# Reordering the softmax's VectorE work and the weight conversion in a fused attention and expert kernel

## The chip, the cores and the metric

One core of one Trainium2 chip runs the whole kernel in one launch. The metric is the device time of an execution in microseconds (us); the kernel before took 818.86 us, the median of three runs (818.68 to 821.95).

## The reference

Three parts, in fp32: a windowed attention, a mixture of experts with one expert per token, and a dense layer pair with g = h - tanh(h). Shapes: q, k, v are (4, 8, 576, 64); 2304 tokens of width 512; 8 experts of inner width 1024; the last pair has an inner width of 2048.

```python
# attention: each row sees itself and the 63 rows before it
scores = scale * np.matmul(q, k.transpose(0, 1, 3, 2))
scores = np.where(mask, scores, -1000000000.0)
scores = scores - np.max(scores, axis=-1, keepdims=True)
attn = np.exp(scores)
attn = attn / (np.sum(attn, axis=-1, keepdims=True) + 1e-09)
x = np.matmul(attn, v)                      # then (B*S, H*D)
# experts
logits = x @ w_gate + modality_bias[modality_id]
e_idx = np.argmax(logits, axis=1)           # gate_w = softmax(logits)[e_idx]
out[mask] = gate_w[mask, None] * (np.maximum(x[mask] @ w1[e], 0.0) @ w2[e])
# last pair; its weights come as float64
h = x @ w_in
return (h - np.tanh(h)) @ w_out
```

## The kernel before

The instructions are issued in the order in which the Python code runs (a manual schedule); each engine works through its own queue in that order and waits at the head for what it needs. SP issues the direct DMAs, one queue in order.

**Attention.** `attention` (L370) runs an iteration for each of 36 groups g of four 128x128 score blocks, nine per batch, as a software pipeline: in iteration g TensorE gets the transposes of q and k for a later group (`prep`, every second group), the scores of group g+2 (`stS`), the transposes of the probabilities of group g (`stT`) and the product with v of group g-1 (`stV`). In `stS` VectorE takes the row maxima nm of a group from PSUM (L314) and ScalarE computes four exponentials into P with the row sums as an accumulator output (L316; the trace shows each as an ACTIVATE and an ACTIVATION_READ_ACCUMULATOR). In `stN` VectorE adds 1e-9 to the sums (smm, L323) and takes the reciprocal rc (L324), and GpSimd multiplies P by it (L325). In `stT` four transposes go into ps_t, a PSUM pool with one buffer, and PT is copied out by ScalarE for odd g (L335) and by VectorE for even g (L337). The score pool has two buffers, P three. The routing of a finished batch (`route_task`) and the rows for the experts (`xrow_task`) are generators; `Sched.pump` moves every waiting one a step, once per iteration.

**Conversion.** `conv_task` (L698) is one more generator, driven by `conv_step`: it turns the float64 weights of the last pair into two fp32r parts, in 32 tiles. Of each tile ScalarE converts the low words (`conv_low`, L767), VectorE does four operations on the high words (`conv_top`, L757 to L760), GpSimd adds the two (`conv_sum`, L773), and the sum is split by ScalarE (L778) and a VectorE subtraction (L782). Ten tiles (NWA) are converted in attention, the split of each in the steps of the next tile; the others in the expert loop, when ScalarE does the first of the four operations (L755).

**Routing table.** After the last batch `unit_table` (L605) computes on VectorE where each expert's tokens lie. It ends with a flag okB, a 1x1 value that TensorE multiplies by ones (L691) to bring it to 128 partitions; VectorE reads the product (L692 to L695: okc, no, slot). The product uses `xps`, the ring of PSUM buffers that the transposes of gathered tokens (`xsplit`, L838) use too, two buffers in this stage. okc and slot are read only by `out_ids` (L940).

**Expert loop.** `moe` (L957) runs 40 steps p, eight inner slices f for each of five units of tokens. A step loads and splits weights (`wload`, `wsplit`), runs the first layer for slice f (`l1`) and the second for f-1 (`l2`), pumps the generators twice and steps the conversion up to twice, for p from CONV0 = 3 and f from 1 to 6. `xsplit` for the next unit stands in the step with f = 7. At p = N - 7 the conversion's buffers are closed and those for the first chunk of the last stage are opened; `ychunk` then loads it through the ring r, which the weights use too. `second` is the last stage.

Of the kernel before, what the change touches and what calls it, by code (L numbers as in the profile page):

```python
# [8 lines left out]
F32 = mybir.dt.float32  # L9
F32R = mybir.dt.float32r  # L10
BF16 = mybir.dt.bfloat16
I32 = mybir.dt.int32
ALU = mybir.AluOpType
AF = mybir.ActivationFunctionType
AX = mybir.AxisListType
# [26 lines left out]
NWA = 10  # L42
NWB = 7
CONV0 = 3
CONVF = (1, 2, 3, 4, 5, 6)
GATHER0 = 2
XACT = 11
# [28 lines left out]
class Kernel:  # L76
# [218 lines left out]
    def stS(self, g):  # L295
        nc = self.nc
        b, hp, half = self.gl(g)
        ps = self.psS.tile([128, 4, 128], F32, name="ps_s")
        mask = self.mF if half == 0 else self.mG
        nc.tensor.matmul(  # L300
            ps.rearrange("p a b -> p (a b)"), self.idB, mask.rearrange("p a b -> p (a b)"), start=True, stop=True
        )
        for j in range(4):
            if hp is None:
                lhs, rhs = self.qbt[:, j, :], self.kTt[b % 2][:, j, :]
            else:
                i = 4 * half + j
                w = 64 * max(i - 1, 0)
                lhs, rhs = self.qbd[(b * 4 + hp) % 2][:, i, :], self.kT[(b * 4 + hp) % 2][:, w : w + 128]
            nc.tensor.matmul(ps[:, j, :], lhs, rhs, start=False, stop=True, skip_group_check=True)  # L310
        nm = self.at.tile([128, 4], F32, name="nm", bufs=3)
        sm = self.at.tile([128, 4], F32, name="smm", bufs=3)
        P = self.at.tile([128, 4, 128], F32, name="P", bufs=3)
        nc.vector.tensor_reduce(nm, ps, op=ALU.max, axis=AX.X, negate=True)  # L314
        for j in range(4):
            nc.scalar.activation(P[:, j, :], ps[:, j, :], AF.Exp, bias=nm[:, j : j + 1], accum_out=sm[:, j : j + 1])  # L316
        self.grp[g] = [P, sm, None]

    def stN(self, g):
        nc = self.nc  # L320
        P, sm, _ = self.grp[g]
        rc = self.at.tile([128, 4], F32, name="rc", bufs=3)
        nc.vector.tensor_scalar(sm, sm, 1e-9, None, op0=ALU.add)  # L323
        nc.vector.reciprocal(rc, sm)  # L324
        nc.gpsimd.tensor_tensor(P, P, rc[:, :, None].to_broadcast([128, 4, 128]), op=ALU.mult)  # L325

    def stT(self, g):
        nc = self.nc
        P = self.grp[g][0]
        pt = self.psT.tile([128, 4, 128], F32, name="ps_t")  # L330
        for j in range(4):
            nc.tensor.transpose(pt[:, j, :], P[:, j, :], self.idF)  # L332
        PT = self.at.tile([128, 4, 128], F32, name="PT", bufs=2)
        if g % 2:
            nc.scalar.activation(PT, pt, AF.Copy)  # L335
        else:
            nc.vector.tensor_copy(PT, pt)  # L337
        self.grp[g][2] = PT

    def stV(self, g):  # L340
# [29 lines left out]
    def attention(self):  # L370
        NG = 9 * B
        self.load_qk(0)
        self.consts()
        for t in self.qbd + [self.qbt]:
            self.nc.vector.memset(t, 0.0)
        self.consts_route()
        self.load_v(0)
        self.load_qk(1)
        self.prep(0)
        for g in range(-2, NG + 2):  # L380
            n = g + 3
            self.useZ = g < NG
            if 0 < n < NG:
                b, i = divmod(n, 9)
                if i < 8 and i % 2 == 0:
                    pi = 4 * b + i // 2
                    self.prep(pi)
                if i == 5:
                    self.prep_tail(b)
                if n == 1:  # L390
                    self.sched.add(self.consts_gate())
                if n == 4:
                    self.conv = self.conv_task()
                if i < 8 and i % 2 == 1:
                    pi = 4 * b + i // 2
                    self.shift_v(pi)
                    if pi + 2 < 4 * B:
                        self.load_qk(pi + 2)
                    if pi + 1 < 4 * B:
                        self.load_v(pi + 1)  # L400
            if 0 <= g + 1 < NG:
                self.stN(g + 1)
            if 0 <= g + 2 < NG:
                self.stS(g + 2)
            if 0 <= g < NG:
                self.stT(g)
            if 0 <= g - 1 < NG:
                self.stO(g - 1, self.stV(g - 1))
                if (g - 1) % 9 == 8:
                    self.sched.add(self.route_task((g - 1) // 9))  # L410
            if g >= NG - 2:
                u, f = self.units["E", 0], g - NG + 2
                if f < 3:
                    self.wload(u, f, 1)
                if f >= 2:
                    self.wload(u, f - 2, 2)
                if f == 2:
                    self.wsplit(u, 0, 1)
            self.sched.pump()
            if g % 3 != 2 or g < 6:  # L420
                self.conv_step()


# [181 lines left out]
    def unit_table(self):  # L605
        nc, rt = self.nc, self.rt
        v = nc.vector
# [3 lines left out]
        n = self.counts("nB")  # L611
# [14 lines left out]
        g = rt.tile([1, NLIST, E], F32, name="le")[:, :E]  # L626
# [59 lines left out]
        self.fin = fin  # L686
        okB = rt.tile([1, 1], BF16, name="okB")
        v.tensor_scalar(okB, over, float(NSTAT), None, op0=ALU.is_le)
        yield 2
        ps = self.xps([128, 1])  # L690
        nc.tensor.matmul(ps, self.ones[0:1, :], okB, start=True, stop=True)  # L691
        v.tensor_copy(self.okc, ps)  # L692
# [5 lines left out]
    def conv_task(self):  # L698
        tiles = [(0, f) for f in range(NF2)] + [(1, f) for f in range(NF2)]
        ready = lambda w, f: (f < NWA or self.conv_on) if w == 0 else f < len(self.woutH) or self.woutW  # L700
        raws, late = [self.conv_load(*t) for t in tiles[:2]], None
        for _ in range(5):
            yield
        for i, (w, f) in enumerate(tiles):
            while not ready(w, f):
                yield
            cur = raws.pop(0)
            r = self.conv_low(cur)
            if i < NWA:
                if late:  # L710
                    hl = self.split_hi(*late)
                yield
                if late:
                    self.split_lo(hl, late[2])
                a = self.conv_top(cur, False)
            else:
                a = self.conv_top(cur, True)
                if late:
                    self.split(*late)
                yield  # L720
            late = self.conv_sum(w, f, a, r)
            if i + 2 < len(tiles):
                raws.append(self.conv_load(*tiles[i + 2]))
            yield
        if late:
            self.split(*late)
        self.conv_done = True
# [17 lines left out]
            nc.sync.dma_start(raw, ap["wout"].bitcast(I32)[f * 128 : f * 128 + 128, :])  # L745
        return raw

    def conv_top(self, raw, act):

        hi = raw.rearrange("p (n two) -> p n two", two=2)[:, :, 1]  # L750
        a = self.cv.tile([128, 512], I32, name="cva")
        v, x = self.nc.vector, a.bitcast(F32)
        hf = raw.bitcast(F32).rearrange("p (n two) -> p n two", two=2)[:, :, 1]
        if act:
            self.nc.scalar.activation(x, hf, AF.Abs)  # L755
        else:
            v.tensor_scalar(a, hi, 0x7FFFFFFF, None, op0=ALU.bitwise_and)  # L757
        v.tensor_scalar(x, x, bits(0x38000000), bits(0x47EFFFFF), op0=ALU.max, op1=ALU.min)
        v.tensor_scalar(a, a, 0x07FFFFFF, 3, op0=ALU.bitwise_and, op1=ALU.logical_shift_left)
        v.scalar_tensor_tensor(a, hi, -0x40000000, a, op0=ALU.bitwise_and, op1=ALU.bitwise_or)  # L760
        return a

    def conv_low(self, raw):
# [193 lines left out]
    def moe(self):  # L957
        order = [("E", j) for j in range(NEARLY)] + list(range(NSTAT))
        seq = [(u, f) for u in order for f in range(NF1)]
        N = len(seq)  # L960
# [5 lines left out]
        for p in range(N):  # L966
            self.conv_on = True
            i, f = p // NF1, p % NF1
# [5 lines left out]
            u, g = at(p + 3)  # L974
# [4 lines left out]
            u, g = at(p + 2)  # L979
            if u is not None:  # L980
                self.wload(u, g, 2)
            u, g = at(p + 1)
            if u is not None:
                self.wsplit(u, g, 1)
            u, f = at(p)
# [6 lines left out]
            elif p == N - 4:  # L992
                self.sched.add(self.out_ids())
            self.sched.pump()
            if f in CONVF and p >= CONV0:
                self.conv_step()
            if f:
                if f == NF1 - 1 and p + 1 < N:
                    self.xsplit(U[seq[p + 1][0]], 2)
                self.l2(u, f - 1)  # L1000
            self.sched.pump()
            if f in CONVF and p >= CONV0:
                self.conv_step()
            if f == NF1 - 1:
                if p + 1 < N:
# [3 lines left out]
            if 1 <= f <= 4 and i > 0 or p == N - 1:  # L1009
                j = i - (p < N - 1)  # L1010
# [3 lines left out]
            if p == NF1 + 1:  # L1014
# [4 lines left out]
                self.woutH += [wc.tile([128, DM], F32R, name=f"woutH{f}") for f in range(NWB, half)]  # L1019
                self.woutL += [wc.tile([128, DM], F32R, name=f"woutL{f}") for f in range(NWB, half)]  # L1020
                self.woutW = [wc.tile([128, DM], I32, name=f"woutW{f}") for f in range(half)]
            if p == N - 7:
                assert not self.conv
                self.es_cv.close()
                y0, self.es_y0 = self.pool("y0", 1)
                self.ybuf = [self.ytiles(y0, 0)]
                self.yc = {}
                self.sched.add(self.ychunk(0, self.mo, "r"))
# [277 lines left out]
def bits(x):  # L1306
    return struct.unpack("<f", struct.pack("<I", x))[0]
# [35 lines left out]
```

## Time and profile before

| | before |
|---|---|
| median of three runs | 818.86 us |
| the profiled execution | 820.09 us, its span 818.3 us |
| TensorE (PE) busy | 763.6 us, 93% of the span |
| VectorE (DVE) busy | 638.6 us, 78% |
| ScalarE (ACT) busy | 527.6 us, 64% |
| GpSimd (POOL) busy | 262.4 us, 32% |

The profile is one execution. Busy time is the union of an engine's instructions; PEld, the weight loads, overlaps PE. A line L314 is line 314 of the kernel. An idle time in brackets is that of the engine just before the instruction, with the instruction that ended it. A row of the windows view gives a stretch, its length, then the busy time of PE, PEld, VectorE, ScalarE and GpSimd in this order. The granted clock is a mean over a stretch, 1.00 being 2.4 GHz. Attention lasts until about 160 us, the expert loop from about 171 to 402 us, and the last stage to the end.

### The profile page before, as it was taken

The page shows a single profiled execution, that of the slowest core. Times are in us where ns is not written, and L with a number is a line of the kernel's source. Part 1 is how long each engine was busy: PE and PEld are TensorE (multiplying, and loading weights), DVE is VectorE, ACT ScalarE, POOL GpSimd, SP SyncE. Part 2 cuts the span into 40 slices and gives each one's busy share as a digit, 9 for nine tenths or more (in the row PEclk, how much of TensorE's full clock was granted, in tenths as well). Part 3 has the DMA queues.
Part 4 walks back from the last instruction along what each step waited for, and adds up shares of the span by engine and source line. Part 5 has one row for each costly group of instructions (what it writes and reads, how often), then busy time and mean ns, then how long its engine had stood idle before and what let it go on. Part 6 is the DMA issues. An engine that isn't in the chain of part 4 may idle for free.

```text
span 818.3 us, 13365 instructions
## 1 busy us (share of the span) xinstructions
PE 763.6 (93%) x4462; PEld 658.5 (80%) x4478; DVE 638.6 (78%) x1137; ACT 527.6 (64%) x1250; POOL 262.4 (32%) x271
## 2 busy tenths in 40 slices
PE   7798889789789999999899999999999999999995
PEld 5677676657578888889889999999999999999993
DVE  4658687756968788775499888888888888888883
ACT  4867676735445565545588777777777767777772
POOL 4333333520105142331024343323424423334223
PEclk9999999899989999999999999999999999999998
DMA  6867867455338586664400010100101101000001
GB/s 137 200 164 179 208 157 200 147 171 174 111 104 262 179 240 203 196 192 144 134 1 29 10 40 10 30 14 26 40 1 40 33 7 39 21 2 26 14 1 42
DMA packets 114543, 80.38 MB, mean 98 GB/s; under 512 B 66141, under 2 KB 102511, under 8 KB 114465
## 3 DMA queue, kind: packets, MB, share of 16 engines
q1 hardware_dynamic: 111201, 69.81, 30.1%
q0 software_dynamic: 3264, 9.63, 3.8%
q8 instruction: 37, 0.61, 0.3%
q14 instruction: 41, 0.34, 0.1%
HBM read 62.10 MB, written 14.16 MB: 93 GB/s over the span
## 4 chain that ended last, share of the span: by engine, by line
PE 79%; DVE 8%; ACT 5%; DMA 3%; issue 2%; POOL 1%; SPq 0%; POOLq 0%; ACTq 0%; DVEq 0%
PE ps_g L1155 24%; PE ps_q L1198 23%; PE ps_h L880 10%; PE ps_y L897 10%; ACT P L316 2%; PE ps_s L310 2%; DMA qr<-in_q 2%; PE ps_o L354 1%; PE ps_t L332 1%; PE x L838 1%; PE x L453 1%; DVE nm L314 1%; PE z L453 1%; DMA r<-yd 1%; PE x L430 1%
## 5 line engine op out<-in xcount | busy, mean ns | idle before, releaser
L1186 POOL TENSOR_TENSOR gl<-gv,gh 128x384 fp32r<-128x384 f32 x96 | 99.8, 1039 | 214.6 <-ACT gh L1185 214.2
L1155 PE MATMUL ps_g<-yh,winH 128*128 128x384 f32 x384 | 129.6, 338 | 2.0 <-DVE gt L1176 2.0
L1155 PE MATMUL ps_g<-yl,winH 128*128 128x384 f32 x384 | 129.6, 337 | 0.0
L1155 PE MATMUL ps_g<-yh,winL 128*128 128x384 f32 x384 | 129.3, 337 | 0.0
L1177 DVE COPY_PREDICATED gv<-gm,gt 128x384 f32<-128x384 int32 x96 | 109.4, 1139 | 10.2 <-ACT gu L1167 0.5
L1198 PE MATMUL ps_q<-woutH,gl 128*128 128x512 f32 x288 | 113.5, 394 | 1.0 <-POOL gl L1186 1.0
L1198 PE MATMUL ps_q<-woutL,gh 128*128 128x512 f32 x288 | 113.5, 394 | 0.0
L1198 PE MATMUL ps_q<-woutH,gh 128*128 128x512 f32 x288 | 113.0, 392 | 0.1
L1185 ACT ACTIVATE gh<-gv 128x384 fp32r<-128x384 f32 x96 | 50.3, 524 | 96.8 <-issue 81.9
L1173 DVE SCALAR_TENSOR_TENSOR gv<-gu,ps_g 128x384 f32<-128x384 f32 x96 | 53.1, 553 | 36.7 <-ACT gt L1170 36.2
L1155 PEld LDWEIGHTS ps_g<-yh,winH 128*128 128x128 f32 x384 | 72.1, 188 | 6.6 <-DVE gt L1176 2.6
L1155 PEld LDWEIGHTS ps_g<-yl,winH 128*128 128x128 f32 x384 | 72.1, 188 | 3.8
L1175 DVE SCALAR_TENSOR_TENSOR gv<-gs,gv 128x384 f32<-128x384 f32 x96 | 72.4, 755 | 3.3
L773 POOL TENSOR_TENSOR cvw<-cva,cvr 128x512 int32<-128x512 int32 x24 | 36.0, 1498 | 114.8 <-DVE winL L782 50.8
L316 ACT ACTIVATE P<-ps_s,nm 128x128 f32<-128x128 f32 x144 | 51.0, 371 | 33.3 <-DVE nm L314 30.9
L1155 PEld LDWEIGHTS ps_g<-yh,winL 128*128 128x128 f32 x384 | 72.1, 188 | 0.0
L1198 PEld LDWEIGHTS ps_q<-woutL,gh 128*128 128x128 f32 x288 | 54.0, 188 | 12.2
L1198 PEld LDWEIGHTS ps_q<-woutH,gl 128*128 128x128 f32 x288 | 54.1, 188 | 10.5 <-POOL gl L1186 1.7
L1168 ACT ACTIVATE gs<-gu,pa 128x384 f32<-128x384 f32 x96 | 59.3, 618 | 4.4 <-DVE gv L1174 1.2
L1174 DVE SCALAR_TENSOR_TENSOR gv<-gs,gv 128x384 f32<-128x384 f32 x96 | 58.8, 612 | 3.3
L1198 PEld LDWEIGHTS ps_q<-woutH,gh 128*128 128x128 f32 x288 | 54.0, 188 | 9.1 <-ACT gh L1185 0.5
L1169 ACT ACTIVATE gs<-gu,pa 128x384 f32<-128x384 f32 x96 | 57.9, 604 | 3.5 <-DVE gv L1175 3.5
(263 smaller groups left out, 1653.9 us busy)
## 6 DMA issues: line engine op xcount, KB each, us to landing
r<-in_w SPq DMA_DIRECT2D x80, 256.0 KB
raw<-in_win SPq DMA_DIRECT2D x16, 512.0 KB
raw<-in_wout SPq DMA_DIRECT2D x16, 512.0 KB
xs<-r SPq DMA_DIRECT2D x18, 256.0 KB
kr<-in_k SPq DMA_DIRECT2D x32, 128.0 KB
qr<-in_q SPq DMA_DIRECT2D x32, 128.0 KB
va<-in_v SPq DMA_DIRECT2D x32, 128.0 KB
yd<-ys SPq DMA_DIRECT2D x16, 252.0 KB
```

The lines of the kernel that those rows point to most:

```text
L316: nc.scalar.activation(P[:, j, :], ps[:, j, :], AF.Exp, bias=nm[:, j : j + 1], accum_out=sm[:, j : j + 1])
L880: nc.tensor.matmul(ps, w[:, c, :], x[:, c, :n], start=(c == 0 and i == 0), stop=(c == 3 and i == 2))
L897: nc.tensor.matmul(u.y[d], w[:, d * 128 : d * 128 + 128], x, start=(f == 0 and i == 0), stop=(f == NF1 - 1 and i == 2),)
L1155: nc.tensor.matmul(ps, w[:, c, :], x[:, c, :], start=(c == 0 and i == 0), stop=(c == 3 and i == 2))
L1168: nc.scalar.activation(s1, u, AF.Square, bias=self.pa1)
L1169: nc.scalar.activation(s2, u, AF.Square, bias=self.pa2)
L1173: nc.vector.scalar_tensor_tensor(v, u, cA, ps, op0=ALU.mult, op1=ALU.mult)
L1174: nc.vector.scalar_tensor_tensor(v, s1, b1, v, op0=ALU.add, op1=ALU.mult)
L1175: nc.vector.scalar_tensor_tensor(v, s2, b2, v, op0=ALU.add, op1=ALU.mult)
L1177: nc.vector.copy_predicated(v, m.bitcast(I32), t)
L1186: nc.gpsimd.tensor_tensor(gl, v, gh.bitcast(F32), op=ALU.subtract)
L1198: nc.tensor.matmul(self.po[t], g[:, sl], w, start=(f == 0 and i == 0), stop=(f == NF2 - 1 and i == 2))
```

## The change

In `attention` the scores of group g+2, with their maxima and exponentials, are issued ahead of the sums of group g+1; the conversion is stepped once between `stN` and `stT` of every iteration, and at the end of an iteration when g is not a multiple of 4 (before: at the end of two in three). For the first ten tiles `conv_top` is issued in two parts in two steps, and the split in two steps of the same tile. The exponentials have no accumulator output; `stN` sums P with one VectorE reduction. PT is always copied by ScalarE. `unit_table` waits 14 pumps instead of 2 before it multiplies the flag. In the expert loop the conversion is not stepped at p = 9 and 10, and also at f = 0 from the third unit on; its buffers are closed one step later.

```diff
@@ stS, stN, stT
-            nc.scalar.activation(P[:, j, :], ps[:, j, :], AF.Exp, bias=nm[:, j : j + 1], accum_out=sm[:, j : j + 1])
+            nc.scalar.activation(P[:, j, :], ps[:, j, :], AF.Exp, bias=nm[:, j : j + 1])
...
+        nc.vector.tensor_reduce(sm, P, op=ALU.add, axis=AX.X)
         nc.vector.tensor_scalar(sm, sm, 1e-9, None, op0=ALU.add)
...
-        if g % 2:
-            nc.scalar.activation(PT, pt, AF.Copy)
-        else:
-            nc.vector.tensor_copy(PT, pt)
+        nc.scalar.activation(PT, pt, AF.Copy)
@@ attention
+            if 0 <= g + 2 < NG:
+                self.stS(g + 2)
             if 0 <= g + 1 < NG:
                 self.stN(g + 1)
-            if 0 <= g + 2 < NG:
-                self.stS(g + 2)
+            self.conv_step()
             if 0 <= g < NG:
                 self.stT(g)
...
-            if g % 3 != 2 or g < 6:
+            if g % 4:
                 self.conv_step()
@@ unit_table
-        yield 2
+        yield 14
         ps = self.xps([128, 1])
@@ conv_task
             if i < NWA:
-                if late:
-                    hl = self.split_hi(*late)
+                a = self.conv_top(cur, False, 1)
                 yield
-                if late:
-                    self.split_lo(hl, late[2])
-                a = self.conv_top(cur, False)
+                self.conv_top(cur, False, 2, a)
             else:
                 a = self.conv_top(cur, True)
                 if late:
                     self.split(*late)
-                yield
+            yield
             late = self.conv_sum(w, f, a, r)
             if i + 2 < len(tiles):
                 raws.append(self.conv_load(*tiles[i + 2]))
             yield
+            if i < NWA:
+                hl = self.split_hi(*late)
+                yield
+                self.split_lo(hl, late[2])
+                late = None
+                yield
@@ conv_top: part 1 is L757 (or L755) and L758, part 2 is L759 and L760
...
@@ moe
-            if f in CONVF and p >= CONV0:
+            if f in CONVF and p >= CONV0 and p not in CONVN:
                 self.conv_step()
...
-            if f in CONVF and p >= CONV0:
+            if (f in CONVF or f == 0 and i > 1) and p >= CONV0 and p not in CONVN:
                 self.conv_step()
...
-            if p == N - 7:
+            if p == N - 6:
```

CONVN is (9, 10).

## Rows read from the trace of the kernel before

**Rows 1.** Windows: busy us (count) by engine, granted clock, DMA share, GB/s

```profile
10.00:160.00 150.00, 127.57 (x1281) 103.23 (x1296) 107.84 (x286) 106.89 (x411) 56.25 (x64) 0.94 0.71 175
...
240.00:380.00 140.00, 140.00 (x654) 115.97 (x653) 111.25 (x172) 78.29 (x143) 43.13 (x29) 1.00 0.65 198
380.00:415.00 35.00, 30.98 (x209) 29.57 (x208) 20.95 (x37) 20.53 (x43) 5.51 (x5) 1.00 0.41 135
```

**Rows 2.** The same view, two stretches of 10 us that hold stalls

```profile
150.00:160.00 10.00, 7.50 (x58) 5.79 (x57) 7.95 (x24) 6.17 (x23) 6.40 (x6) 0.66 0.52 152
220.00:230.00 10.00, 3.61 (x15) 2.62 (x14) 8.69 (x28) 1.77 (x3) 1.58 (x1) 0.57 0.51 154
```

**Rows 3.** Waits in attention: engine, line, releaser; total us, times, longest

```profile
ACT P L316 <- DVE nm L314: 27.2, 18, 3.3
...
DVE smm L323 <- ACT P L316: 14.0, 17, 1.6
...
PE ps_t L332 <- ACT PT L335: 10.6, 8, 2.7
...
PE ps_t L332 <- POOL P L325: 4.6, 4, 2.1
```

**Rows 4.** Timeline near 110 us: start, us, instruction, idle before, releaser

```profile
108.41 0.43 DVE L759 TENSOR_SCALAR cva<-cva 128x512 int32<-128x512 int32 x1
...
108.88 0.69 DVE L760 SCALAR_TENSOR_TENSOR cva<-raw,cva 128x512 int32<-128x512 int32 x1
...
109.49 0.16 DVE L323 TENSOR_SCALAR smm<-smm 128x4 f32<-128x4 f32 x1
...
109.85 0.66 DVE L314 TENSOR_REDUCE nm<-ps_s 128x4 f32<-128x512 f32 x1
...
110.60 0.37 ACT L316 ACTIVATE P<-ps_s,nm 128x128 f32<-128x128 f32 x1 [3.29 <-DVE nm L314]
110.87 0.19 ACT L316 ACTIVATION_READ_ACCUMULATOR P<-ps_s,nm 128x1 f32 x1
...
110.96 0.36 ACT L316 ACTIVATE P<-ps_s,nm 128x128 f32<-128x128 f32 x1
...
111.98 0.61 ACT L335 ACTIVATE PT<-ps_t 128x512 f32<-128x512 f32 x1
...
112.74 0.63 PE L332 MATMUL ps_t<-idF,P 128*128 128x128 f32 x4 [2.41 <-ACT PT L335]
```

**Rows 5.** Groups of instructions in attention: count, busy us, mean ns, idle before

```profile
L314 DVE TENSOR_REDUCE nm<-ps_s 128x4 f32<-128x512 f32 x36 | 24.2, 672 | 10.8 <-PE ps_s L310 10.5 <-issue 0.3
...
L337 DVE COPY PT<-ps_t 128x512 f32<-128x512 f32 x18 | 12.3, 685 | 2.3 <-PE ps_t L332 2.3
```

**Rows 6.** The chain of waits near 31 and 36 us: start, us, what

```profile
31.43 0.44 PE ps_t L332 x4
31.87 0.62 PE ps_o L354 x16
...
35.82 0.32 PE ps_s L300
36.14 0.90 PE ps_s L310 x8
```

**Rows 7.** The timeline at 121 us

```profile
120.98 1.27 POOL L773 TENSOR_TENSOR cvw<-cva,cvr 128x512 int32<-128x512 int32 x1 [3.83 <-DVE cva L760]
...
121.32 0.95 DVE L323 TENSOR_SCALAR smm<-smm 128x4 f32<-128x4 f32 x1
```

**Rows 8.** The timeline of the table's product, then the chain of waits after it

```profile
222.94 0.16 PE L691 MATMUL x<-okB,ones 1*128 1x1 bf16 x1 [2.46 <-DVE okB L688]
...
227.20 0.67 DVE L886 SCALAR_TENSOR_TENSOR hl<-ps_h,hh 128x504 fp32r<-128x504 f32 x1
...
228.05 1.10 PE L838 MATMUL x<-idF,xg 126*128 126x126 f32 x4 [3.93 <-DVE no L694]
...
233.94 2.75 PE ps_y L897 x12
```

More of the change, by code (lines that the diff above doesn't have):

```diff
@@ L44 @@
 CONV0 = 3
+CONVN = (9, 10)
 CONVF = (1, 2, 3, 4, 5, 6)
@@ L746, in conv_load, with conv_top @@
         return raw
-    def conv_top(self, raw, act):
+    def conv_top(self, raw, act, part=3, a=None):
         hi = raw.rearrange("p (n two) -> p n two", two=2)[:, :, 1]
-        a = self.cv.tile([128, 512], I32, name="cva")
+        if part & 1:
+            a = self.cv.tile([128, 512], I32, name="cva")
         v, x = self.nc.vector, a.bitcast(F32)
[L753 to L760, printed above, removed]
+        if part & 1:
+            if act:
+                hf = raw.bitcast(F32).rearrange("p (n two) -> p n two", two=2)[:, :, 1]
+                self.nc.scalar.activation(x, hf, AF.Abs)
+            else:
+                v.tensor_scalar(a, hi, 0x7FFFFFFF, None, op0=ALU.bitwise_and)
+            v.tensor_scalar(x, x, bits(0x38000000), bits(0x47EFFFFF), op0=ALU.max, op1=ALU.min)
+        if part & 2:
+            v.tensor_scalar(a, a, 0x07FFFFFF, 3, op0=ALU.bitwise_and, op1=ALU.logical_shift_left)
+            v.scalar_tensor_tensor(a, hi, -0x40000000, a, op0=ALU.bitwise_and, op1=ALU.bitwise_or)
         return a
```

## The prediction

> **What bounds the kernel now.** I began with the totals of the profile's page: TensorE is busy for 93% of the span, so some 55 us of it are idle, and the question is where. Cut by stage [rows 1], the stretch from 240 to 380 us has no idle at all (140.00 of 140), so what the change does to the conversion there is free as long as it stays under TensorE. The idle lies in attention (10 to 160 us: 150 - 127.57 = 22.4 us), then around the routing table, and in the hand-over to the last stage (380 to 415: 4.0 us). The clock adds to it: over attention the mean granted clock is 0.94, so 0.06 x 150 = 9 us of full clock are missing, and in two 10 us stretches with long stalls it was 0.66 and 0.57 [rows 2], part of each at 1.2 instead of 2.4 GHz.
>
> Next, who ends the waits in attention [rows 3]: TensorE waits 10.6 us for the ScalarE copy of PT and 4.6 us for GpSimd's scaled P, 15.2 us together. Behind them stands ScalarE, which waits 27.2 us for the row maxima nm, and VectorE, which waits 14.0 us for the exponentials before it may add to the sums. One such place in order of time [rows 4]: the conversion's L759 and L760 end at 109.57, the small add L323 follows them, nm only starts at 109.85, the first exponential at 110.60 after 3.29 us of idle ScalarE, the PT copy at 111.98, and TensorE transposes at 112.74 after 2.41 us of idle. So attention is limited by VectorE's order, not by an engine that is full: VectorE is busy for 107.84 of 150 us, ScalarE for 106.89 [rows 1].
>
> Around the table [rows 8] TensorE waits 2.46 us for okB, then 3.93 us until VectorE has read that product (L694), since the next transposes need its PSUM buffer: 6.4 us.
>
> **The change part by part.** The sum is made against the profiled execution, 820.1 us (span 818.3 and 1.8 around it); that run lies 1.2 us above the median of the runs shown, 818.9.
>
> *Order of maxima and sums, pieces of the conversion.* nm(g+2) now stands ahead of the sums of group g+1, so it no longer waits for Exp(g+1) (the 14.0 us of [rows 3]), and the VectorE run ahead of it is shorter. The conversion was issued as one run of four operations, three like L759 (0.43 us) and L760 (0.69 us) [rows 4], about 2 us, after the subtraction for the tile before; now the first two (0.86 us) and the last two (1.12 us) are apart. It is five steps per tile, one step between the sums and the transposes of every iteration and one at the end of three iterations in four: 7 steps in 4 iterations. Ten tiles and five empty steps need 55, so it ends at iteration 31, where the old one ended its tenth tile at 34 and left a split for later. I value this as 60% of the 15.2 us: -9. Both ends: 0 (the wait only moves) and -15.2. I don't take all of it, because an iteration that gets both pieces still has 2 us of conversion, and VectorE carries more (next).
>
> *Sums on VectorE.* 36 reductions are added. No row shows this one; nm has its shape but reads PSUM, 672 ns [rows 5]. Bounds: 0.43 us and 0.69 us, the shortest and the longest of the conversion's operations on 512 columns in SBUF [rows 4], 15 to 25 us; I take nm's 672 ns, 24.2 us. Removed are 18 PT copies of 685 ns [rows 5], 12.3 us. Net +11.9 us: 119.7 us of VectorE work, 80% of the old 150 us and 85% of a stretch of 141. Its cover is VectorE's idle 42 us. Where a group's nm finds VectorE still busy it is late and TensorE pays; that is the other reason for 60%.
>
> *No accumulators on ScalarE.* 144 reads go. Exponentials started at 110.60 and 110.96, the read between them at 110.87 [rows 4]: the read holds the engine for 0.09 us, 0.36 per group, 13 us in all. Bound on the one side: nothing, if the exponentials are paced by something else and start 0.36 apart without a read too; on the other: with the read goes the wait for the sum itself, and an exponential follows as soon as a quarter of the 512-column copy would (112.74 - 111.98 = 0.76 us at most for that copy and its hand-over, so 0.19), 0.17 x 144 = 24 us. The path nm, Exp, PT gets shorter by about 0.36 us; I count that below.
>
> *All PT copies on ScalarE.* Eighteen more of 0.6 to 0.7 us, some 12 us on an engine that saves 13: even. But T(g+1) needs the one ps_t buffer back, so it now waits each time behind four exponentials, and also behind a conversion step of ScalarE (issued between them). From the start of nm to T it was 112.74 - 109.85 = 2.89 us [rows 4], without the reads 2.53. TensorE meanwhile has T, V and the next S with its mask, 0.44 + 0.62 + 0.32 + 0.90 = 2.28 us [rows 6], and over a microsecond more where the q and k transposes come between. So about 0.3 us in 18 of 36 groups, 5 us, of which I count 2 within the 40% that stays, and more where the conversion's step comes first: I take +3. Ends: 0 and, at 0.7 us for each of the 36, +25.
>
> *Clock.* With the long stalls shortened, some of the low-clock time goes: -2.5, which is less than what the stretch at 150 us alone lost (0.34 x 10) [rows 2]. Ends: 0 and -9.
>
> Attention: -9 + 3 - 2.5 = -8.5.
>
> *Flag product later.* The product moves 12 pumps, six steps of the expert loop, to where TensorE is full and okB long made. TensorE's 6.4 us go, but not all is gained. VectorE's queue there is unchanged: hl ends at 227.87 [rows 8]. Without the flag TensorE goes on at 222.94 - 2.46 = 220.5 with two transposes (1.1 us) and the 12 products of the second layer (2.75 us), until about 224.4. The third transpose needs the first's PSUM buffer, which is free when xl, behind that hl, ends: 227.9 + 0.6 = 228.5. Then two transposes and 12 products, 1.3 + 2.75, and the stage ends near 233 instead of 236.7. So -3.5; ends 0 (if VectorE's queue runs later) and -6.4.
>
> *Expert loop and hand-over.* No conversion at two steps, more at f == 0: VectorE has 140 - 111 = 29 us free there [rows 1], nothing. The buffers for the last stage open one step later, so its first loads share SP's queue and the ring r with the last weights. The old order already lost 4.0 us there [rows 1]; I take 0, ends -1 and +2.
>
> Sum: -8.5 - 3.5 + 0 = -12. 820.1 - 12 = 808.1 for the profiled run, less 1.2 for the median: 807.
>
> **A rule that speaks against it.** In [rows 7] the small add L323, 0.16 us in [rows 4], took 0.95 us at 121.32 while GpSimd ran cvw from 120.98 to 122.25. The Trainium skill (SBUF — State Buffer, "SBUF: two separate sides") says that VectorE and GpSimd share one port pair as an exclusive lock, which whoever starts first holds for a whole instruction, against VectorE operations in a two-port mode or with two SBUF inputs; the trace agrees, with these 0.95 us. It matters here: before, a maximum that reads PSUM followed the reciprocal that starts GpSimd's multiplication; now a conversion piece follows it.
>
> **Rivals.**
> 1. *VectorE is filled up and nothing is won in attention.* About 17 conversion steps (ten tiles, three of five steps with VectorE work, 57% in the middle place) follow the reciprocal while GpSimd multiplies; at 0.95 - 0.16 = 0.79 us each [rows 4, 7] that is 13 us, and with +11.9 VectorE holds 133 of 150 us. Its bursts then give the stalls back. For it: VectorE's 80% without them. Against: the piece may start before GpSimd does, and then GpSimd waits, which has an iteration of slack. Only the table gains: 820.1 - 3.5 - 1.2, 815 to 817.
> 2. *Slower: the single ps_t buffer.* Every T waits for a ScalarE copy behind four exponentials; it decides as soon as Exp(g+2) ends later than S(g+3). At 0.7 us for 36 groups +25, less today's 10.6 for the odd groups, and -3.5 for the table: +11, 830. For it: today's waits are all on ScalarE's copies, none on VectorE's [rows 3]. Against: those waits follow a late nm, as in [rows 4], which the change moves forward.
> 3. *All goes well.* Attention loses all 15.2 us and 9 of clock, the table 6.4: -31, 788.
>
> **How the numbers follow.** Forecast 0.55 (own range 799 to 814), rival 1 0.20, rival 2 0.17, rival 3 0.08. A measurement of this kernel can't tell less than about 0.5%, 4.1 us, from none. Faster (under 814.8): nearly all of the forecast, rival 3 and a third of rival 1: 0.68. Same: most of rival 1 and the mild part of rival 2: 0.19. Slower: 0.13. The range 796 to 822 leaves out most of rivals 2 and 3, under 0.2.
>
> **What would show it.** Right: ScalarE's waits for nm fall from 27.2 us to under 15; VectorE's waits for P nearly vanish; TensorE's waits for PT and P fall from 15.2 to about 9; the mean clock of attention rises above 0.95; the table wait of 2.46 us is gone and one of 3 to 4 us on xl is left; attention ends some 8 us earlier. Wrong: waits of ps_t for PT in nearly every group (rival 2), or VectorE busy for over 90% of attention, with conversion operations of 0.9 us and more in the middle place (rival 1).

## The result and the profile after

The changed kernel takes 832.8 us, the median of four runs (830.72 to 835.39); the kernel before took 820.4 us in the runs beside them. The ratio is 1.0136, its 95% interval 1.0091 to 1.0182: slower by some 11 us, where 12 us less had been forecast. The profiled execution took 831.77 us, its span 829.9 us.

Cut at the first product of the expert loop and at the first of the last stage, the two profiled executions compare so (us, from their timelines):

| | before | after | difference |
|---|---|---|---|
| until the expert loop's first product | 171.6 | 177.9 | +6.3 |
| expert loop, the table's place included | 231.1 | 236.3 | +5.2 |
| last stage, to the end of the span | 415.6 | 415.7 | +0.1 |

So there are two losses, one in each of the first two stages. The windows of the kernel after, to be set beside [rows 1, 2]; the columns are the same:

```profile
10.00:160.00 150.00, 119.41 (x1237) 96.38 (x1246) 126.49 (x294) 101.70 (x280) 56.37 (x62) 0.99 0.70 172
60.00:155.00 95.00, 74.62 (x772) 60.07 (x778) 83.54 (x201) 62.71 (x170) 35.16 (x38) 0.98 0.69 174
240.00:380.00 140.00, 136.35 (x618) 111.35 (x617) 101.92 (x163) 72.53 (x132) 40.39 (x28) 1.00 0.62 193
380.00:415.00 35.00, 30.09 (x202) 29.27 (x201) 18.89 (x35) 15.86 (x34) 5.60 (x5) 0.90 0.44 128
150.00:160.00 10.00, 5.26 (x64) 4.43 (x66) 9.48 (x25) 5.73 (x19) 6.40 (x7) 1.00 0.42 126
```

VectorE holds 126.49 of the 150 us from 10 to 160 us, 84% (before 107.84), and 88% of the steady middle, 83.54 of 95. The expert loop, which had no idle on TensorE, now has 3.65 us of it in 140. The clock of attention did rise, from 0.94 to 0.99, and the stage is longer all the same.

The waits in attention (15 to 155 us) of the kernel after, against [rows 3]:

```profile
ACT P L317 <- DVE nm L315: 29.2, 26, 3.4
...
PE ps_t L334 <- POOL P L327: 15.6, 15, 2.2
...
DVE nm L315 <- PE ps_s L311: 9.6, 9, 2.1
...
PE ps_t L334 <- ACT PT L336: 3.6, 4, 1.6
```

TensorE's wait has changed its releaser: 10.6 us for PT and 4.6 for P before, 3.6 and 15.6 now, 19.2 instead of 15.2. GpSimd's scaled P is late because the reciprocal is (the multiplication starts 0.17 us after the reciprocal's end in nearly every group), and the reciprocal because VectorE is. ScalarE's wait for the maxima, which was to fall under 15 us, stands at 29.2. VectorE's wait for the exponentials is gone, as forecast, and the stage is no shorter for it. The groups of VectorE, same stretch (columns as in [rows 5]):

```profile
L315 DVE TENSOR_REDUCE nm<-ps_s 128x4 f32<-128x512 f32 x32 | 21.7, 680 | 9.6 <-PE ps_s L311 9.6
L324 DVE TENSOR_REDUCE smm<-P 128x4 f32<-128x512 f32 x32 | 21.6, 674 | 0.0
L766 DVE SCALAR_TENSOR_TENSOR cva<-raw,cva 128x512 int32<-128x512 int32 x10 | 12.0, 1195 | 0.3
L763 DVE TENSOR_SCALAR cva<-cva 128x512 f32<-128x512 f32 x10 | 7.9, 787 | 0.3
```

The sum costs 674 ns, which was forecast to 2 ns. The third and fourth rows are rival 1's lock: L766 took 693 ns on average before and takes 1195 now, L763 427 and 787. They are L760 and L758 of the kernel before, same stretch:

```profile
L760 DVE SCALAR_TENSOR_TENSOR cva<-raw,cva 128x512 int32<-128x512 int32 x9 | 6.2, 693 | 0.3
...
L758 DVE TENSOR_SCALAR cva<-cva 128x512 f32<-128x512 f32 x9 | 3.8, 427 | 0.3
```

The timeline of one group of the kernel after shows both the sum and the lock:

```profile
65.67 0.68 DVE L315 TENSOR_REDUCE nm<-ps_s 128x4 f32<-128x512 f32 x1
...
66.28 0.67 DVE L324 TENSOR_REDUCE smm<-P 128x4 f32<-128x512 f32 x1
66.45 1.14 ACT L317 ACTIVATE P<-ps_s,nm 128x128 f32<-128x128 f32 x4 [0.43 <-DVE nm L315]
...
67.19 0.18 DVE L326 RECIPROCAL rc<-smm 128x4 f32<-128x4 f32 x1
67.28 0.40 DVE L765 TENSOR_SCALAR cva<-cva 128x512 int32<-128x512 int32 x1
...
67.54 1.04 POOL L327 TENSOR_TENSOR P<-P,rc 128x512 f32<-128x512 f32 x1 [2.60 <-DVE rc L326]
67.71 1.41 DVE L766 SCALAR_TENSOR_TENSOR cva<-raw,cva 128x512 int32<-128x512 int32 x1
...
68.63 0.66 PE L334 MATMUL ps_t<-idF,P 128*128 128x128 f32 x4 [1.10 <-POOL P L327]
...
71.05 0.66 DVE L315 TENSOR_REDUCE nm<-ps_s 128x4 f32<-128x512 f32 x1
...
71.81 0.37 ACT L317 ACTIVATE P<-ps_s,nm 128x128 f32<-128x128 f32 x1 [3.45 <-DVE nm L315]
```

The sum stands ahead of the reciprocal, so P starts some 0.7 us later than it would without it; L766 is stretched past the end of GpSimd's multiplication at 68.58; VectorE goes on with the routing's small operations without a gap, and the next maximum starts only at 71.05, so that ScalarE has been idle for 3.45 us when it goes on. Which of the three is to blame (the sum's place, the lock, or the amount of work) this can't say; the experiments had to.

In the expert loop, TensorE's waits of the kernel after:

```profile
PE x L927 <- DVE eqa L924: 6.6, 3, 3.1
PE x L844 <- DVE xl L847: 4.4, 1, 4.4
```

The wait for okB (2.46 us, [rows 8]) is gone and one of 4.4 us on xl is left, where 3 to 4 us were forecast. The 6.6 us on eqa are new: a cast that `put_ids` needs. The timeline of the kernel after around one:

```profile
302.48 1.07 PE L903 MATMUL ps_y<-hl,w2h 128*128 128x504 f32 x4
...
302.92 0.69 DVE L788 TENSOR_TENSOR woutL<-cvw,woutH 128x512 fp32r<-128x512 f32 x1
303.52 0.69 DVE L877 TENSOR_TENSOR w1l<-r,w1h 128x512 fp32r<-128x512 f32 x1
...
304.12 1.75 DVE L877 TENSOR_TENSOR w2l<-r,w2h 128x512 fp32r<-128x512 f32 x1
...
306.39 0.15 DVE L924 CAST eqa<-ids 126x4 f32<-126x4 int32 x1
...
306.69 0.27 PE L927 MATMUL x<-idF,eqa 126*4 126x126 f32 x1 [3.14 <-DVE eqa L924]
```

VectorE has the conversion's operations and both weight splits queued ahead of the small cast, and TensorE, in order, waits for it.

### The profile page after: what moved, and what is told of

It reads as the page before. It is cut to its first block, busy times and chain, and to the rows that moved or that the text cites. A ratio compares the mean times of both kernels' runs of the same rounds, so it can differ in the third digit from the quotient of the medians.

```text
span 829.9 us, 13242 instructions
## 1 busy us (share of the span) xinstructions
PE 760.9 (92%) x4468; PEld 656.0 (79%) x4478; DVE 658.2 (79%) x1155; ACT 524.1 (63%) x1124; POOL 263.7 (32%) x271
## 4 chain that ended last, share of the span: by engine, by line
PE 72%; DVE 19%; ACT 3%; issue 3%; POOL 2%; DMA 1%; SPq 0%; POOLq 0%; DVEq 0%; ACTq 0%
PE ps_g L1161 24%; PE ps_q L1204 23%; PE ps_h L886 10%; PE ps_y L903 9%; DVE nm L315 2%; DVE smm L324 2%; DVE cva L766 1%; DVE w2l L877 1%; DVE cva L763 1%; PE ps_s L311 1%; DVE winL L788 1%; PE x L844 1%; ACT P L317 1%; PE x L453 1%; DVE cva L765 1%
## 5 line engine op out<-in xcount | busy, mean ns | idle before, releaser
L317 ACT ACTIVATE P<-ps_s,nm 128x128 f32<-128x128 f32 x144 | 41.3, 373 | 34.7 <-DVE nm L315 34.5
L327 POOL TENSOR_TENSOR P<-P,rc 128x512 f32<-128x512 f32 x36 | 39.8, 1106 | 71.8 <-DVE rc L326 30.6
L1204 PEld LDWEIGHTS ps_q<-woutH,gl 128*128 128x128 f32 x288 | 54.0, 188 | 10.5 <-POOL gl L1192 1.7
```

What stands on the lines that cost most here:

```text
L1204: nc.tensor.matmul(self.po[t], g[:, sl], w, start=(f == 0 and i == 0), stop=(f == NF2 - 1 and i == 2))
```

## The experiments

Ratios are against the kernel before in the same series of runs (its medians there were 822.1 to 823.1 us), with 95% intervals. Line numbers shift by a few between kernels. "After" is 1.0136 [1.0091, 1.0182].

### Which part is the loss

**e2_sums_undone**: accumulators and alternating PT copies back, all else as after.

```diff
-AF.Exp, bias=nm[:, j : j + 1])
+AF.Exp, bias=nm[:, j : j + 1], accum_out=sm[:, j : j + 1])
-        nc.vector.tensor_reduce(sm, P, op=ALU.add, axis=AX.X)
-        nc.scalar.activation(PT, pt, AF.Copy)
+        (ScalarE for odd g, VectorE for even g)
```

> The changed kernel with the row sums as accumulators of the exponentials again and PT copied alternately. Theory A (the VectorE sum stands on the path from nm to the scaled P, and that path ends TensorE's waits): the waits of ps_t for P fall from 15.6 us to under 6, the first layer of the experts starts 12 us or more earlier than 177.9, and the total is 816 to 822. Theory B (the port lock: conversion pieces run while GpSimd multiplies): the conversion's operations stay at 0.8 to 1.2 us, attention keeps most of its length, the total stays above 826. Theory C (VectorE's load alone): it gives back the 12 us of VectorE work at the rate of the stalls, some 6 us, 826.

829.07 us, 1.0074 [1.0041, 1.0106]: 5.1 us back, so theory A is out. The number lies where theory B, the lock, put it (above 826, the conversion's operations as long as after), but e7 below has the same long operations and takes 823.2 us, so this run does not show the lock to be the cause.

**e3_sums_alone**: the converse, the kernel before with only these two edits.

> The kernel before with only the sums on VectorE and every PT copy on ScalarE; order and conversion as before. Theory A and C: sum and reciprocal and then nm are in series on VectorE, 0.6 us more in each of 36 groups ahead of nm and P: 10 to 20 us slower than before, 830 to 840. Theory B: no conversion piece stands behind the reciprocal, so little changes, 818 to 824.

832.74 us, 1.0128 [1.0074, 1.0182]: this pair alone costs as much as the whole change, 10.5 us. In the new order, from e2 to after, the same pair costs 5.1 us.

**e7_accum_only**: after with the accumulators back and the sum gone; PT stays on ScalarE.

> The changed kernel with the row sums as accumulator outputs again, every PT copy still on ScalarE. If the VectorE sum is what costs (undoing sum and copies together gave 4 us), the first layer of the experts starts near 174, as with both undone, and the waits of T are for PT. If the single ps_t buffer and the ScalarE copies cost (rival 2 of the prediction), the waits of T for PT rise to 20 us and more and the time is that of the changed kernel or longer.

823.2 us, 1.0019 [1.0, 1.0038]. The sum alone is thus worth 1.0136 - 1.0019, 9.6 us; and from e2 to e7, where 18 PT copies leave VectorE, the time falls by another 0.55%, 4.5 us, although ScalarE carries them. Waits of TensorE in e7, 15 to 155 us:

```profile
PE ps_t L333 <- ACT PT L335: 15.1, 16, 1.6
...
PE ps_t L333 <- POOL P L326: 3.0, 2, 1.9
```

**e1_loop_undone**: the conversion's steps and the closing in `moe` as before.

```diff
-            if f in CONVF and p >= CONV0 and p not in CONVN:
+            if f in CONVF and p >= CONV0:
-            if (f in CONVF or f == 0 and i > 1) and p >= CONV0 and p not in CONVN:
+            if f in CONVF and p >= CONV0:
-            if p == N - 6:
+            if p == N - 7:
```

> The changed kernel with the old placement of the conversion in the expert loop (and the old step at which its buffers close). Theory: about 9 of the 12 us lost come from the loop, where the extra conversion step at f = 0 shifts each tile by half a step, so that VectorE reaches the cast of the token ids some 3 us late at three places; then the time falls by 7 to 10 us to 823 to 826 and the waits of TensorE for eqa (3.1, 0.5, 3.0 us) go. Rival: those waits come from the conversion's tile count or from the later flag, not from the placement; then it stays within 2 us of 832.8.

826.45 us, 1.0052 [1.0026, 1.0077]: 6.9 us back, and the expert loop of the profile falls by as much (236.3 to 229.4 us); TensorE's waits for eqa are gone.

**e4_order_undone**: after with `stN` ahead of `stS` again.

> The changed kernel with the sums of group g+1 ahead of the maxima of g+2 again; pieces, VectorE sums and PT as changed. Theory A: P is ready earlier by the time of nm, its waits fall by half, but ScalarE's waits for nm rise; total 826 to 833. Theory B: nm, which reads PSUM, now stands between the reciprocal and the conversion piece and covers 0.6 of GpSimd's 1.04 us, so the pieces are locked out by at most 0.4 us: total 822 to 827. Forecast's reasoning (the order is a gain): 5 us or more slower, above 837.

837.07 us, 1.0183 [1.0125, 1.024]. The median is 4 us worse than after, at the edge of what the forecast's reasoning asked for (above 837), but the intervals overlap: the new order is no loss here, and perhaps a gain of some 4 us.

### The sum: its place, the lock, or the load

**e6_step_between**: the conversion's middle step moved between `stS` and `stN`, so that no piece follows the reciprocal.

```diff
             if 0 <= g + 2 < NG:
                 self.stS(g + 2)
+            self.conv_step()
             if 0 <= g + 1 < NG:
                 self.stN(g + 1)
-            self.conv_step()
```

> The changed kernel with one edit: the conversion step in the middle of an iteration stands between the maxima of g+2 and the sums of g+1, no longer behind the reciprocal that starts GpSimd. Lock theory: the conversion's operations fall from 1195, 787, 575 ns back to about 693, 427, 437 ns, VectorE is relieved of some 10 us, and attention ends 4 to 8 us earlier (825 to 829). Path theory (nm, sum, reciprocal, GpSimd, T): the piece now lies on the path of P in some iterations, TensorE's waits for P grow from 15.6 us by as much as the lock gives back, and the time stays within 3 us of the changed kernel or rises.

836.86 us, 1.0186 [1.0149, 1.0223]. The operation that had been stretched to 1195 ns is back at its length of before:

```profile
L766 DVE SCALAR_TENSOR_TENSOR cva<-raw,cva 128x512 int32<-128x512 int32 x10 | 6.9, 692 | 0.3
```

L763 (643 ns) and L788 (804) are not, so that some 7 of the 11 us by which GpSimd's lock stretched the conversion are gone, not all. Nothing is won. TensorE waits longer for P, 20.8 us where it waited 15.6:

```profile
PE ps_t L334 <- POOL P L327: 20.8, 17, 2.0
```

The piece now stands ahead of the reciprocal, which may be why; what the lock would be worth with the same order can't be read from this.

**e14_load_ahead** and **e13_load_behind**: e7 with an added reduction of a constant 128x512 tile per group, whose result is unused; in the one ahead of the addition and the reciprocal, where the sum was, in the other behind the reciprocal and the conversion's step.

```diff
+        dm = self.at.tile([128, 4], F32, name="dm", bufs=3)
+        nc.vector.tensor_reduce(dm, idF (repeated four times), op=ALU.add, axis=AX.X)
```

> The same unused reduction, but ahead of the add and the reciprocal, where the changed kernel has its sum; accumulators kept. Path theory: as the changed kernel, 830 to 835, with TensorE's waits for P of 12 us or more; slower than the same work behind by 4 us or more. Load theory: the same as the one behind, within 2 us.

> The kernel with accumulators only (823.2) plus a reduction of 512 columns of a constant on VectorE in every group, behind the reciprocal and the conversion step; its result is not used, so it is VectorE work that is on nobody's data path. Load theory: VectorE is as full as in the changed kernel, the time is 830 to 833. Path theory (the cost is that nm, sum and reciprocal stand in series ahead of P): 824 to 828, TensorE's waits for P well under 15 us.

832.09 us, 1.0099 [1.0067, 1.0131] ahead; 834.5 us, 1.0127 [1.0085, 1.0169] behind. Off the way to P the same 24 us of work cost no less: the path theory wanted the one ahead 4 us or more slower, and it is 2.4 us faster, within overlapping intervals. The first fence has the added group, the waits and the window of 60 to 155 us of e14, the second those of e13:

```profile
L325 DVE TENSOR_REDUCE dm<-idF 128x4 f32<-128x512 f32 x36 | 24.3, 675 | 0.0
...
ACT P L317 <- DVE nm L315: 20.2, 20, 2.9
...
PE ps_t L335 <- ACT PT L337: 10.2, 10, 1.6
...
PE ps_t L335 <- POOL P L328: 9.4, 9, 1.7
...
60.00:155.00 95.00, 75.33 (x776) 60.23 (x782) 80.80 (x202) 70.78 (x255) 35.28 (x38) 0.98 0.68 172
```

```profile
L406 DVE TENSOR_REDUCE dm<-idF 128x4 f32<-128x512 f32 x36 | 23.9, 664 | 0.0
...
ACT P L317 <- DVE smm L324: 21.8, 14, 3.3
PE ps_t L333 <- ACT PT L335: 19.0, 18, 2.1
...
60.00:155.00 95.00, 74.27 (x782) 59.65 (x789) 81.24 (x195) 69.51 (x249) 31.92 (x36) 1.00 0.66 168
```

Only the name of the wait differs: P, or PT by way of a late nm. (Where the second fence has ScalarE wait for the add L324, nm ended just ahead of that add: 87.74 + 0.67 = 88.41, the exponential at 88.50.)

```profile
87.74 0.67 DVE L315 TENSOR_REDUCE nm<-ps_s 128x4 f32<-128x512 f32 x1
...
88.33 0.15 DVE L324 TENSOR_SCALAR smm<-smm 128x4 f32<-128x4 f32 x1
...
88.50 0.37 ACT L317 ACTIVATE P<-ps_s,nm 128x128 f32<-128x128 f32 x1 [1.52 <-DVE smm L324]
```

VectorE is 85% full in both; in e7 it is 80%:

```profile
60.00:155.00 95.00, 78.43 (x840) 63.44 (x849) 75.89 (x200) 76.04 (x279) 40.80 (x43) 1.00 0.72 182
```

### The expert loop, and a better version

**e10_best_between** (accumulators, alternating PT, the old loop, the flag, the pieces, the step as in e6) and **e11_best_oldorder** (the same, with the step behind the reciprocal and `stN` ahead of `stS`):

> Maxima ahead, pieces and the later flag, but accumulators, alternate PT copies and the old placement in the expert loop, with the middle step between maxima and sums. From the parts: the loop 229.5 as with its placement undone, attention near before's 171.6 or better if the lock was what the new order lost; 812 to 820. If the order itself costs (P late behind nm) attention stays near 175 and the total at 820 to 823.

> The same, but with the sums ahead of the maxima as in the kernel before and the middle step behind the maxima: only the pieces and the flag are left of the change. If the shorter conversion runs are the gain and the order is the loss, attention ends at 165 to 170 and the total is 812 to 817, the fastest of these; if the order is the gain, as forecast, it is slower than the one with the maxima ahead by 3 us or more.

820.36 us, 0.9981 [0.9959, 1.0004], and 818.45 us, 0.9945 [0.9917, 0.9972]. With the accumulators the maxima's place ahead of the sums shows no gain of its own (the two differ in the step's place as well). e10 lies where its text put a costly order (820 to 823), e11 just above its 812 to 817.

**e12_combined**: after with both losses undone, that is e7 with e1's edit; PT stays on ScalarE, the maxima, the pieces and the flag as in the change. **e15_combined_between**: the same with the step as in e6.

> Maxima ahead, pieces, every PT on ScalarE and the later flag, with accumulators and the old placement in the expert loop: attention as with accumulators only (first layer near 169.5, after 177.9 of the change) and the loop as with its placement undone (229). If the parts add: 823.2 - 6 = 817, 0.5% faster than before. If the loop's gain needs the other attention or the two overlap: 820 to 823.

> As the combination, with the middle step between maxima and sums, so out of the lock. Lock theory: 2 to 5 us faster than the combination. Path theory: the add and the reciprocal come later by the piece, 0 to 4 us slower; alternate copies and this place gave 820.4.

814.68 us, 0.9883 [0.984, 0.9926], and 815.82 us, 0.9927 [0.9893, 0.9961]. e12 beats both kernels, and lies 2 us under the 817 that adding the parts gave. Its wait and its window of 60 to 155 us:

```profile
PE ps_t L333 <- ACT PT L335: 16.0, 16, 1.6
...
60.00:155.00 95.00, 78.67 (x842) 63.73 (x850) 76.13 (x204) 74.61 (x271) 40.71 (x43) 0.98 0.71 180
```

e15 has its operations out of the lock in part (L765 692 ns instead of 1195, L762 571 instead of 714) and gains nothing either, where the lock theory wanted 2 to 5 us. It differs from e10 in the PT copies alone and repeats what e2 and e7 showed of them: 0.9981 to 0.9927, 4.4 us gained.

**e17_half_step**: e12 with a single additional step of the conversion, at p = 16. **e18_close_later**: e12 with the buffers closed one step later. **e19_flag_undone**: e12 with 2 pumps ahead of the flag.

```diff
e17 -            if f in CONVF and p >= CONV0:
    +            if (f in CONVF or p == 16) and p >= CONV0:
e18 -            if p == N - 7:
    +            if p == N - 6:
e19 -        yield 14
    +        yield 2
```

> The combination (814.7) with one extra conversion step at p = 16, f = 0, and nothing else of the change's loop edits. Half-step theory: from there each tile's steps stand the other way round in a step p, VectorE reaches the cast of token ids late, TensorE waits for it at the third unit (3 us) and, the old placement going on, also at the fourth; the loop grows by 3 us or more, to 817.5 or above. Rival (the wait comes from skipping p = 9 and 10 or from the later close): loop as in the combination, 813 to 816.

> The combination with the conversion's buffers closed, and those of the last stage opened, one step p later. The prediction took this as 0 (-1 to +2). If the later loads of the first chunk hold ScalarE's queue at the end of the loop it is 2 us or more slower, 817 and above; else within 1 us of 814.7.

> The combination with the flag product after 2 pumps again. If the later flag is worth what the traces of the loops say (231.1 and 232.7 us with it early, 227.7 to 229.6 late), it is 2 to 4 us slower, 817 to 819, with TensorE's waits of 2.5 us for okB and 3.9 us for L694 back and the wait of 4.4 us for xl gone.

e17: 822.77 us, 0.9979 [0.9956, 1.0002], 8 us more than e12. e18: 814.11 us, 0.9878 [0.9835, 0.992], no difference. e19: 819.14 us, 0.995 [0.9932, 0.9969], so the flag's later product is worth 4.5 us by the medians, 5.5 by the ratios, of which the expert loop of the profiles shows 3.3 (229.6 to 232.9 us). TensorE's old waits are back in e19:

```profile
PE x L843 <- DVE no L693: 3.9, 1, 3.9
PE x L690 <- DVE okB L687: 2.4, 1, 2.4
```

Of the 8 us of e17's one step, 5.3 stand in the expert loop of its profile (229.6 to 234.9 us): a tile takes two steps in the loop, and from p = 16 on the one with VectorE's operations falls into the other half of each p. The rest stands in attention, where the edit changes nothing and the profile is 3.7 us longer than e12's; its cause is open. The same instructions of attention took from 167.9 to 171.6 us in the profiles of e7, e12, e17, e18 and e19, so a difference of a few us between two profiles of attention shows nothing by itself. Waits of TensorE in e17's loop, then 250 to 385 us of e12 and of e17:

```profile
PE x L926 <- DVE eqa L923: 5.0, 2, 3.1
PE x L843 <- DVE xl L846: 4.4, 1, 4.4
```

```profile
250.00:385.00 135.00, 135.00 (x667) 113.61 (x667) 102.59 (x162) 71.69 (x132) 38.58 (x26) 1.00 0.66 199
```

```profile
250.00:385.00 135.00, 130.05 (x617) 107.57 (x616) 100.69 (x160) 71.23 (x131) 36.39 (x26) 1.00 0.65 195
```

The waits on eqa come with the half step and are absent without it. In e12 the cast ran at 294.44, ahead of the conversion's operations at 294.74, and TensorE had it in time.

## Why the prediction was wrong

**The failing step is "Its cover is VectorE's idle 42 us."** Idle time of an in-order engine is no cover when the work stands in the queue ahead of the next maximum: nm, Exp, P, PT and T form a loop from group to group, and what is put into VectorE's turn of that loop comes out of it in part. The load itself was forecast well: 85% of VectorE, and 84% came. It was the cover that failed, and with it "So attention is limited by VectorE's order, not by an engine that is full". Four measurements in the new order put the price near each other. The sums: 24.2 us of work, 9.6 us of time (0.40). The unused reduction: 24.3 us for 6.6 ahead, 23.9 us for 8.9 behind (0.27 and 0.37). The PT copies that left: 12.3 us for 4.5 (0.37). Each of these times is uncertain by 3 to 4 us. A fifth does not fit: in the old order, with the conversion in one run, the pair of e3 cost 10.5 us for its net 11.9 us of work, nearly 0.9. The theory that the sum hurts by standing ahead of the reciprocal fell with e13. That the loop from nm to T carries the price is read from the timelines; the runs show the price and that the place does not lower it.

**60% of 15.2 us for the order.** At most half of the 9 us shows, and only while the sums are on VectorE: some 4 us in e4, within overlapping intervals, and the pair that costs 10.5 us in the old order (e3) costs 5.1 in the new (e2). With the accumulators back, e10 and e11 show none. The wait of VectorE for the exponentials went, as the row promised; it was idle time of an engine that then had more to do.

**Accumulators off ScalarE.** The reads went (101.70 us of ScalarE instead of 106.89, with 18 more PT copies), and four exponentials take 1.14 us where they started 0.36 us apart. ScalarE waits for nm instead. Time saved on ScalarE had been bought with time on VectorE, the dearer engine.

**PT on ScalarE, +3, and rival 2.** The wrong sign: 4.5 us gained between e2 and e7, 4.4 between e10 and e15. In e7 and e12 the transposes T do wait for PT in nearly half of the groups (16 times, 1.6 us at most), which rival 2 foresaw, but VectorE's relief is worth more.

**The lock, rival 1.** The mechanism is there at nearly the forecast size: (502 + 360 + 135 + 131) ns, the excess of L766, L763, L762 and L788 over their means of before in the groups of 15 to 155 us, times ten tiles is 11.3 us, against 13. The Trainium skill (SBUF — State Buffer, "SBUF: two separate sides") says that a VectorE operation in a two-port mode, or with two SBUF inputs beside a GpSimd operation that reads SBUF, is blocked for the whole of a GpSimd instruction that started first; this trace agrees: L766, with two inputs, took 1.41 us in the seven tiles in which GpSimd's multiplication ran beside it and 0.69 us in the other three. But rival 1 took the table's 3.5 us as all that moves and ended at 815 to 817. Its "VectorE is filled up" was right, its price of nothing was too low, and no experiment has shown the lock itself to decide: e7 and e12 carry it too (L765 with 1195 ns in both) and stand 1.2% and 2.5% below after, and e6 and e15, which take some 7 us of it away and move the piece, gain nothing. What the lock alone costs stays open.

**Flag, -3.5.** Right: the waits are those named, and e19 gives 4.5 us by the medians, 3.3 of it in the loop.

**Expert loop, 0 with an end of +2.** Wrong by 7 us (e1). I counted VectorE's free 29 us there, as in attention, and did not look at where in each step the conversion's operations fall. The closing of the buffers, which I did worry about, costs nothing (e18).

**Clock, -2.5.** The granted clock rose as said (0.94 to 0.99), and its worth can't be separated here.

So 9.6 us for the sums and 6.9 us for the loop, less the flag's 3.3 to 5.5, come to 11 to 13 us, which are the 11 to 12 us to be explained; that leaves order, pieces, lock and PT together within some 2 us of nothing. e12, which has these four and the flag, gives another account: it is 9.6 us faster than before, which leaves them 4 to 6 us of gain, about what PT gave. The two accounts differ by some 4 us, no more than the intervals allow, and the runs don't say which is nearer.

## What to carry to other kernels

An engine that is 72% busy and works in order inside a loop between engines is not free for the rest: in the new order each added microsecond of VectorE work cost 0.3 to 0.4 us, in either of two places, and each one removed gave as much back; in the old order it was nearly 0.9. Price added work at a slope measured on the kernel at hand, not at zero, before valuing the waits that it removes. Where a background task takes two steps per item, count which half of the period its heavy step falls into: one step too many shifted all that came after it, and a 0.15 us cast behind it held TensorE for 3 us.

## What the hardware showed that was not expected

Without the accumulator's read four exponentials of 128 columns end 1.14 us after the first starts; at 0.37 us for each, they start about 0.26 us apart, an estimate, against 0.36 with the reads (110.60 and 110.96 in [rows 4]). A 1.04 us GpSimd multiplication starts while VectorE is at work on L765 (67.54, between the starts 67.28 and 67.71 of two operations that follow each other without a gap), and it is the next one, L766, that is stretched: VectorE's full queue did not keep GpSimd out here. The sum, with one SBUF input, shows no sign of the lock: eight of the 36 ran beside a GpSimd operation, and took 0.67 us like the others.
